# Buffers, queues and split places of the transform back in an S4 + MLP block

## The chip, the cores and the metric

One core of a Trainium2 chip runs the whole block in one program. The time is the device time of an execution in microseconds (us), read as the median of several runs. The engines named below are PE (TensorE), DVE (VectorE), ACT (ScalarE), POOL (GpSimd) and SP (SyncE, which here only issues DMAs). A DMA can be issued from SP, ACT or POOL; each has its own queue and issues in program order.

## The reference, cut to what matters

The block takes 2048 tokens of 512 channels, normalises and modulates them, and runs an S4 convolution (a kernel `K` per channel, applied by FFT of length 4096). A second normalisation and modulation is followed by a token-shift mixing (`w1`, gelu, four shifts, `w2`) and a channel MLP (`w3`, gelu, `w4`).

```python
x = A_u
h = layernorm(x) * (1 + ca) + sa
x = x + ga * S4(h)                       # y = irfft(rfft(K) * rfft(h)) + h * Dskip
h = layernorm(x) * (1 + cb) + sb
g = gelu(layernorm(h) @ w1)              # quarters of g shifted by +1, -1, +2, -2 tokens
x1 = h + shifted(g) @ w2
x = x + gb * (x1 + gelu(layernorm(x1) @ w3) @ w4)
```

## The kernel before

The program is written by hand in the order in which each engine runs it (`manual_schedule`); tiles come from pools with a fixed number of buffers, and an instruction that writes a new tile waits until the last use of the tile whose buffer it takes.

**Stage 1** (to about 209 us) computes the kernel `K` in SBUF (`KX`) and the first transform of `h`, which goes to DRAM as `VU`. Beside it POOL copies the weights from the inputs to DRAM scratch (`Dw2`, `Dw3`, `Dw4`).

**Stage 2** (about 209 to 302 us) is the middle of the transforms. `k_first` (eight rounds) makes `VK0` and `VK1`. Then come 16 steps, two halves `jh` of the channels with eight `kc` each. In step n, PE runs `spectrum_k(n)` (64 small products, reading the twiddles `T2` and the negated twiddles `T3`, which POOL writes in `flip`). DVE runs `multiply(n)`: four products (`ma`, `mb`, L690) and two sums (`zc`, L692). PE runs `back(n-1)` (four products with `Gm`); ACT evicts them to `z` (two buffers) and POOL stores `z` to DRAM (`ZT`, two DMAs of 256 KB). PE runs `spectrum_u(n+1)` on a block of `VU` (512 KB) that SP loaded into `ld`, a ring of seven buffers. The same ring holds the two loads of `w1` (512 KB each) and the blocks of the transform back, `load_inv`. SP also loads the four parts of `x` (1024 KB each) into `KX`. In steps 12 and 13 `inverse(0, 0)` and `inverse(0, 3)` use the first four loaded blocks of the first half (k = 0, 3, 4, 7), in step 15 `i1` uses the other four. `w1` and `w2` are split into a high part (ACT, L115) and a low part (DVE, L756) in steps 9, 10, 14 and 15.

**The hole** (about 302 to 314 us): after the last step the last `z` goes to DRAM and the blocks of the second half come back, transposed by the address pattern; only then can PE go on (`py`, L731).

**Stage 3** (about 314 to 374 us) is the rest of the transform back and the mixing. `mix_half(t, hl, hf)` does 24 products for half a pair of token tiles and gelu on ACT (`go`, two buffers), `mix_out` stores `go` to DRAM (`GD`), and `chan_load(g)` loads the shifted windows `win` from there. All these DMAs stand on SP's queue, and so do the loads of `w3` and `w4`. **Stage 4** (to the end) is the channel MLP, eight groups of tiles in `chan`.

## Time and profile before

| | |
|---|---|
| runs | 688.75, 689.73, 693.65 us; median 689.73 us |
| the profiled execution | 691.26 us, its span 689.5 us, mean clock 0.989 |
| PE busy | 642.6 us (93%) |
| DVE busy | 498.0 us (72%) |
| ACT busy | 331.2 us (48%) |
| POOL busy | 124.8 us (18%) |
| DMA | 86.42 MB, mean 125 GB/s |

PE's busy time is a sum over stages with different limits, and its matmuls overlap; the stages are read apart with the view by windows. A row of the timeline gives start, duration, engine, line, operation, output<-input and, in brackets, the idle time just before it and what ended it.

### The profile page before, as it was taken

The page shows a single profiled execution, that of the slowest core. Times are in us where ns is not written, and L with a number is a line of the kernel's source. Part 1 is how long each engine was busy: PE and PEld are TensorE (multiplying, and loading weights), DVE is VectorE, ACT ScalarE, POOL GpSimd, SP SyncE. Part 2 cuts the span into 40 slices and gives each one's busy share as a digit, 9 for nine tenths or more (in the row PEclk, how much of TensorE's full clock was granted, in tenths as well). Part 3 has the DMA queues.
Part 4 walks back from the last instruction along what each step waited for, and adds up shares of the span by engine and source line. Part 5 has one row for each costly group of instructions (what it writes and reads, how often), then busy time and mean ns, then how long its engine had stood idle before and what let it go on. Part 6 is the DMA issues. An engine that isn't in the chain of part 4 may idle for free.

```text
span 689.5 us, 16884 instructions
## 1 busy us (share of the span) xinstructions
PE 642.6 (93%) x7195; PEld 509.2 (74%) x7195; DVE 498.0 (72%) x795; ACT 331.2 (48%) x505; POOL 124.8 (18%) x236
## 2 busy tenths in 40 slices
PE   1899999999999998977998999999999999999996
PEld 0456655655569776634887889999899889898895
DVE  7899999999996887986987967464574536363522
ACT  3878988889875557432444623123131312222121
POOL 4011112112103355413741101001010000000000
PEclk9999999999999999998999999999999999999999
DMA  8603264643739997967387010020100201010001
GB/s 299 284 2 79 75 218 105 209 121 85 275 85 317 354 335 258 346 204 226 108 257 240 1 32 32 16 77 15 47 31 17 77 1 62 1 49 13 1 31 31
DMA packets 51091, 86.42 MB, mean 125 GB/s; under 512 B 4676, under 2 KB 39496, under 8 KB 48424
## 3 DMA queue, kind: packets, MB, share of 16 engines
q1 hardware_dynamic: 46712, 66.74, 30.1%
q0 software_dynamic: 3440, 17.57, 7.4%
q8 instruction: 56, 0.92, 0.6%
q10 hardware_dynamic: 864, 1.05, 0.5%
q14 instruction: 19, 0.16, 0.1%
HBM read 59.12 MB, written 32.90 MB: 133 GB/s over the span
## 4 chain that ended last, share of the span: by engine, by line
PE 70%; DVE 6%; DMA 5%; ACT 3%; POOL 2%; issue 1%; ACTq 0%; SPq 0%; DVEq 0%; POOLq 0%
PE pm L841 7%; PE pm L838 7%; PE pm L839 7%; PE xx L448 7%; PE pa L954 6%; PE pa L955 6%; PE pa L962 6%; PE kp L498 3%; DMA ZT<-z 3%; PE ph L893 2%; PE ph L895 2%; PE ph L892 2%; DMA ld<-ZT 2%; PE pu L426 2%; PE pT L803 2%; PE pk L626 2%
## 5 line engine op out<-in xcount | busy, mean ns | idle before, releaser
L115 ACT ACTIVATE gh<-pm 128x512 fp32r<-128x512 f32 (+1 forms) x48 | 26.9, 560 | 200.7 <-PE pm L841 200.7
L838 PE MATMUL pm<-nh,w3h 128*128 128x256 f32 (+1 forms) x352 | 86.6, 281 | 2.7 <-ACT nh L115 2.7
L839 PE MATMUL pm<-nh,w3l 128*128 128x256 f32 (+1 forms) x352 | 86.3, 280 | 0.1
L946 DVE TENSOR_TENSOR gl<-gf,gh 128x512 fp32r<-128x512 f32 (+1 forms) x48 | 30.8, 643 | 68.4 <-ACT gf L115 68.4
L954 PE MATMUL pa<-w4h,gh 128*128 128x512 f32 (+1 forms) x176 | 69.6, 395 | 0.0
L838 PEld LDWEIGHTS pm<-nh,w3h 128*128 128x128 f32 (+1 forms) x352 | 66.0, 187 | 4.4 <-ACT nh L115 2.9
L955 PE MATMUL pa<-w4l,gh 128*128 128x512 f32 (+1 forms) x176 | 68.9, 392 | 0.0
L839 PEld LDWEIGHTS pm<-nh,w3l 128*128 128x128 f32 (+1 forms) x352 | 65.9, 187 | 2.2 <-DVE w3l L756 0.5
L765 POOL TENSOR_TENSOR rs<-mv,eps_t 128x1 f32<-128x1 f32 (+1 forms) x39 | 11.0, 282 | 282.4 <-DVE mv L771 265.4
L841 PE MATMUL pm<-nl,w3h 128*128 128x256 f32 (+1 forms) x352 | 55.0, 278 | 0.0
L449 PE MATMUL xx<-MG,ON 64*128 64x512 f32 x160 | 48.1, 397 | 0.0
L962 PE MATMUL pa<-w4h,gl 128*128 128x512 f32 (+1 forms) x176 | 48.0, 390 | 0.0
L448 PE MATMUL xx<-MG,ON 64*128 64x512 f32 x160 | 48.0, 396 | 0.0
L841 PEld LDWEIGHTS pm<-nl,w3h 128*128 128x128 f32 (+1 forms) x352 | 47.0, 187 | 0.0
L898 DVE TENSOR_TENSOR h<-h,ph 128x512 f32<-128x512 f32 x16 | 11.0, 687 | 45.1 <-PE ph L895 45.1
L466 DVE SCALAR_TENSOR_TENSOR e<-tr,p 128x512 f32<-128x512 f32 x64 | 41.1, 684 | 1.5 <-ACT tr L115 1.5
L498 PEld LDWEIGHTS kp<-e,e 128*32 128x32 f32 x2048 | 30.1, 110 | 12.7 <-issue 7.6
L475 DVE TENSOR_TENSOR e<-tr,p 128x1024 f32<-128x1024 f32 x32 | 39.0, 1220 | 0.0
L476 DVE TENSOR_TENSOR e<-tr,m 128x1024 f32<-128x1024 f32 x32 | 39.0, 1219 | 0.0
L115 ACT ACTIVATE p<-xx 128x1024 f32<-128x1024 f32 (+1 forms) x40 | 37.5, 979 | 2.2 <-PE xx L252 1.0
L962 PEld LDWEIGHTS pa<-w4h,gl 128*128 128x128 f32 (+1 forms) x176 | 33.0, 188 | 7.3 <-DVE gl L946 0.2
L115 ACT ACTIVATE tr<-xx 128x1024 f32<-128x1024 f32 x32 | 33.0, 1030 | 9.6 <-PE xx L449 7.9
(236 smaller groups left out, 1731.6 us busy)
## 6 DMA issues: line engine op xcount, KB each, us to landing
VU<-vs SPq DMA_DIRECT2D x64, 128.0 KB, 3.7
ld<-VU SPq DMA_DIRECT2D x16, 512.0 KB, 7.4
ZT<-z POOLq DMA_DIRECT2D x30, 256.0 KB, 6.2
ld<-ZT SPq DMA_DIRECT2D x12, 512.0 KB
Dw<-in_w POOLq DMA_DIRECT2D x8, 688.0 KB, 4.7
xu<-in_u SPq DMA_DIRECT2D x4, 1024.0 KB, 8.0
KX<-in_x SPq DMA_DIRECT2D x4, 1024.0 KB, 8.0
GD<-go SPq DMA_DIRECT2D x16, 256.0 KB, 2.3
```

The costliest lines, as they stand in the source:

```text
L115: return S.activation(out, in_, f, bias=bias, scale=scale)
L448: T.matmul(x[:, :512], la, ma, start=(i == 0), stop=(i == len(ops) - 1))
L449: T.matmul(x[:, 512:], lb, mb, start=(i == 0), stop=(i == len(ops) - 1))
L466: V.scalar_tensor_tensor(e0[:, 1, a], tr[:, 1, 0], 1.0 - 2.0 * a, mg[:, a], op0=OP.mult, op1=OP.mult)
L475: V.tensor_mul(e0[:, 0], tr[:, 0, 0:1].to_broadcast([128, 2, 512]), mg)
L498: T.matmul(kp[32 * j:32 * j + 32, (k % 2) * 4 + g], e1[:, r, d], e0[:, r, :, d * 32:d * 32 + 32], start=(r == 0), stop=(r == 1), skip_grou ...
L838: T.matmul(p, wh[:, k, c], hi[k], start=(k == 0), stop=False)
L839: T.matmul(p, wl[:, k, c], hi[k], start=False, stop=False)
L841: T.matmul(p, wh[:, k, c], lo[k], start=False, stop=(k == 3))
L954: T.matmul(acc[i], gh[:m, e, s], W4h[:m, f], start=(f == 0), stop=False)
L955: T.matmul(acc[i], gh[:m, e, s], W4l[:m, f], start=False, stop=False)
L962: T.matmul(acc[i], gl[:m, e, s], W4h[:m, f], start=False, stop=(f == 10))
```

## The change

Six edits, all in stage 2 and around it. (1) `T3` becomes one tile for all twiddles, written by eight POOL instructions ahead of `k_first`; no flip is left in the 16 steps. (2) The `z` buffers go from two to three. (3) The ring `ld` goes from seven buffers to six, and the blocks k = 0, 3, 4, 7 of the first half get a pool of their own, `zi` (four buffers); they are loaded in step 9 instead of 10, the other four in step 12 instead of 13. `VU` is loaded four steps ahead instead of three. (4) The four loads of `x` move from SP's queue to POOL's, in the order 0, 3, 1, 2 in steps 2, 4, 6, 8. `FI` is loaded in `k_first` instead of step 9, and `Gm` takes `FK`'s buffer after `k_first`. (5) `w1` gets a DRAM copy too, is loaded by POOL straight into the tile of its low part in steps 9 and 10; ACT makes the high parts in steps 13 and 14, DVE the low parts in the hole. (6) `w2` is loaded by one SP DMA after the loads of the hole, its high part is made by ACT after `mix_half(1, hl, 0)`, its low part by DVE after `mix_half(2, hl, 0)`. The products on PE are the same.

```diff
-    Gm = c2.tile([128, 2, 64], F32, name="Gm")
-    ldp = a2.enter_context(pool("ldp", bufs=7))
+    ldp = a2.enter_context(pool("ldp", bufs=6))
...
-    def flip(kc):
-        t = t3s[kc] = c2.tile([128, 8, 64], F32, name="T3", bufs=3)
-        for gh in range(2):
-            r = slice(gh * 64, gh * 64 + 64)
-            P.tensor_scalar(t[r], T2[kc // 4][r, kc % 4 * 4:kc % 4 * 4 + 8, 64 - gh * 64:128 - gh * 64], -1.0, None, op0=OP.mult)
+    T3 = s2.tile([128, 32, 64], F32, name="T3", bufs=1)
+    def flip(i):
+        for a in range(0, 16, 8):
+            for gh in range(2):
+                r = slice(gh * 64, gh * 64 + 64)
+                P.tensor_scalar(T3[r, i * 16 + a:i * 16 + a + 8], T2[i][r, a:a + 8, 64 - gh * 64:128 - gh * 64], -1.0, None, op0=OP.mult)
...
-        z = s2.tile([128, 4, 256], F32, name="z")
+        z = s2.tile([128, 4, 256], F32, name="z", bufs=3)
...
-            zis[jh, k] = block()
+            zis[jh, k] = block() if jh or k in (1, 2, 5, 6) else zip_.tile([128, 4, 256], F32, name="zi")
...
     def load_x(g):
-        Y.dma_start(X2[:, g * 4:g * 4 + 4].rearrange("p b d -> p (b d)"), A["x"][g])
+        P.dma_start(X2[:, g * 4:g * 4 + 4].rearrange("p b d -> p (b d)"), A["x"][g])
...
             def split():
                 for j in range(m):
-                    h = hi[:n, i + j, c0:c1]
-                    act(h, w[:n, j])
-                    V.tensor_sub(lo[:n, i + j, c0:c1], w[:n, j], h.bitcast(F32))
+                    act(hi[:n, i + j, c0:c1], w[:n, j])
+                def low():
+                    for j in range(m):
+                        V.tensor_sub(lo[:n, i + j, c0:c1], w[:n, j], hi[:n, i + j, c0:c1].bitcast(F32))
+                return low
...
-            if n + 3 < 16:
-                load_vu(*steps[n + 3])
-            if n % 2 == 0 and n < 14:
-                flip(steps[n + 2][1])
-            if n in (3, 4, 6, 8):
-                load_x(n - 3 if n < 5 else n // 2 - 1)
+            if n + 4 < 16:
+                load_vu(*steps[n + 4])
+            if n in (2, 4, 6, 8):
+                load_x((0, 3, 1, 2)[n // 2 - 1])
+            if n in (9, 10):
+                w1s.append(ldw1(None, n % 9 * 2, 2, q=P))
+            if n in (13, 14):
+                w1s[n - 13] = w1s[n - 13]()
             if n == 9:
-                Y.dma_start(FI, A["FI"].rearrange("p (a b c) -> p a b c", a=32, b=2))
-            if split:
-                split()
-                split = None
-            if n in (8, 9):
-                split = ldw1(two, n % 2 * 2, 2)
-            if n == 10:
                 for k in (0, 3, 4, 7):
                     load_inv(0, k)
             if n == 12:
+                for k in (1, 2, 5, 6):
+                    load_inv(0, k)
                 inverse(0, 0)
-                w2s = [ldw2(None, 2 * i, 2) for i in range(2)]
...
-            if n in (14, 15):
-                w2s.pop()()
...
         for b in (14, 15, 4, 5, 6, 7):
             half_stat(b, 0)
+        for f in w1s:
+            f()
         for k in (1, 2):
             load_inv(1, k)
             load_inv(1, k + 4)
+        w2s = ldw2(None, 0, 4)
...
         mix_half(1, hl, 0)
+        w2s = w2s()
         mix_norm(2)
...
         mix_half(2, hl, 0)
+        w2s()
         chan_split(0)
```

On SP's queue in stage 2 (`VU` to `ld` are the blocks of u, `ZT_61` the first half's blocks of the transform back, `KX<-in_x` the parts of x), the last rows of the 16 steps stand so before:

```order
L724 DMA KX<-in_x 128x2048
L640 DMA ld<-VU 128x4x256 x2
L724 DMA KX<-in_x 128x2048
L750 DMA ld<-in_w 128x2x512
L640 DMA ld<-VU 128x4x256
L1131 DMA FI<-in_FI 128x2048
L750 DMA ld<-in_w 128x2x512
L640 DMA ld<-VU 128x4x256
L721 DMA ld<-ZT_61 128x4x256 x4
L640 DMA ld<-VU 128x4x256 x2
L750 DMA w2l<-Dw_64 128x2x512 x2
L721 DMA ld<-ZT_61 128x4x256 x4
```

And with the change, from the first block of `VU` on:

```order
L534 DMA xu<-in_T 128x2048
L640 DMA ld<-VU 128x4x256 x4
L1106 DMA FI<-in_FI 128x2048
L1108 DMA FK<-in_G 128x128
L640 DMA ld<-VU 128x4x256 x10
L721 DMA zi<-ZT_61 128x4x256 x4
L640 DMA ld<-VU 128x4x256 x2
L721 DMA ld<-ZT_61 128x4x256 x4
```

The loads of `x`, `w1` and `w2` are gone from this stretch of SP's queue; the first four blocks of `ZT_61` still stand ahead of the last two blocks of `VU`.

On POOL in the 16 steps (`T` are the negated twiddles, `ZT<-z` the stores, two to a step), before:

```order
L706 DMA ZT_61<-z 32x2x1024 x4
L662 TENSOR_SCALAR T_3646<-xu 64x512 x2
L706 DMA ZT_61<-z 32x2x1024 x4
L662 TENSOR_SCALAR T_3792<-xu 64x512 x2
L706 DMA ZT_61<-z 32x2x1024 x4
L662 TENSOR_SCALAR T_3949<-xu 64x512 x2
L706 DMA ZT_62<-z 32x2x1024 x4
```

And with the change:

```order
L662 TENSOR_SCALAR T_3079<-xu 64x512 x8
L706 DMA ZT_61<-z 32x2x1024 x4
L724 DMA KX<-in_x 128x2048
L706 DMA ZT_61<-z 32x2x1024 x4
L724 DMA KX<-in_x 128x2048
L706 DMA ZT_61<-z 32x2x1024 x4
L724 DMA KX<-in_x 128x2048
L706 DMA ZT_61<-z 32x2x1024 x4
L724 DMA KX<-in_x 128x2048
L706 DMA ZT_62<-z 32x2x1024 x2
L750 DMA w1l<-Dw_64 128x2x512
```

The flips between the stores are gone, and a load of `x` or `w1` stands in their place.

On ACT in the mixing (`go` are the gelus, `h` the normalised tiles, `nh` the high parts of the transposed tiles), around `mix_half(1, hl, 0)`, with the change:

```order
L115 ACTIVATE go<-pm 128x512
L115 ACTIVATE w2h<-w2l 128x512 x4
L115 ACTIVATE h_4961<-h_4961,nm,rs 128x512 x2
L115 ACTIVATE go<-pm 128x512
L115 ACTIVATE nh_5138<-pT_5128 128x512
```

Before, the row `w2h` does not stand there, and `h` follows the gelu.

## Rows read from the trace of the kernel before

**Rows 1.** View by windows, the head and five stretches
```profile
core 0: us, PE busy (x) PEld busy (x) DVE busy (x) ACT busy (x) POOL busy (x), PEclk, DMA share, GB/s
224.40:302.00 77.60, 70.45 (x1500) 52.08 (x1500) 67.30 (x112) 44.82 (x87) 35.15 (x42) 1.00 0.92 317
224.40:232.00 7.60, 7.12 (x178) 5.93 (x180) 5.38 (x9) 3.75 (x7) 0.00 (x0) 1.00 1.05 392
247.00:259.00 12.00, 12.00 (x273) 9.85 (x267) 11.77 (x20) 6.67 (x13) 8.52 (x10) 1.00 0.93 303
274.00:290.00 16.00, 13.65 (x278) 9.38 (x274) 16.00 (x28) 8.47 (x17) 9.04 (x11) 1.00 1.04 370
430.00:689.50 259.50, 253.88 (x1626) 228.85 (x1624) 125.81 (x208) 58.72 (x109) 14.02 (x36) 1.00 0.10 31
```

**Rows 2.** Timeline of DVE in the 16 steps
```profile
227.31 0.69 DVE L690 TENSOR_TENSOR ma<-pk,us 128x512 f32<-128x512 f32 x1 [2.12 <-PE pk L680]
...
238.42 0.69 DVE L690 TENSOR_TENSOR ma<-pk,us 128x512 f32<-128x512 f32 x1
...
245.29 0.69 DVE L690 TENSOR_TENSOR ma<-pk,us 128x512 f32<-128x512 f32 x1 [3.19 <-ACT us L115]
...
263.19 0.69 DVE L690 TENSOR_TENSOR ma<-pk,us 128x512 f32<-128x512 f32 x1 [2.69 <-ACT us L115]
...
271.48 1.29 DVE L756 TENSOR_TENSOR w1l<-ld,w1h 128x512 fp32r<-128x512 f32 x2 [1.01 <-ACT w1h L115]
...
276.55 1.70 DVE L756 TENSOR_TENSOR w1l<-ld,w1h 128x512 fp32r<-128x512 f32 x2
...
297.15 1.29 DVE L756 TENSOR_TENSOR w2l<-w2l,w2h 128x512 fp32r<-128x512 f32 x2 [0.26 <-ACT w2h L115]
...
301.36 0.69 DVE L692 TENSOR_TENSOR zc<-mb 128x512 f32<-128x512 f32 x1
```

**Rows 3.** Timeline of POOL, two pairs of flips
```profile
238.27 3.14 POOL L662 TENSOR_SCALAR T<-xu 64x512 f32<-64x512 f32 x2
...
256.72 3.10 POOL L662 TENSOR_SCALAR T<-xu 64x512 f32<-64x512 f32 x2
```

**Rows 4.** Timeline of ACT, two evictions to z
```profile
261.09 1.09 ACT L115 ACTIVATE z<-pz 128x512 f32<-128x512 f32 x2 [4.34 <-DMA ZT<-z]
...
268.38 1.08 ACT L115 ACTIVATE z<-pz 128x512 f32<-128x512 f32 x2 [1.93 <-DMA ZT<-z]
```

**Rows 5.** View of the tile ZT, 224 to 330 us, all its DMAs
```profile
DMA to landing us min/median/max: 2.6/6.0/8.9
```

**Rows 6.** Timeline of SP's queue, the first blocks of ZT
```profile
269.70 4.17 SPq L721 DMA_DIRECT2D ld<-ZT  x4
```

**Rows 7.** Chain of waits, the first use of these blocks
```profile
283.84 1.86 PE pz L731 x32
```

**Rows 8.** The page's DMA issues: KB each, median us to landing
```profile
KX<-in_x SPq DMA_DIRECT2D x4, 1024.0 KB, 8.0
```

**Rows 9.** Timeline of ACT in the mixing
```profile
348.54 1.72 ACT L115 ACTIVATE h<-h,nm,rs 128x512 f32<-128x512 f32 x2
350.81 0.60 ACT L115 ACTIVATE go<-pm 128x512 f32<-128x512 f32 x1 [0.55 <-PE pm L841]
...
374.67 2.20 ACT L115 ACTIVATE w4h<-w4l 128x512 fp32r<-128x512 f32 x4
```

**Rows 10.** Timeline of DVE in the mixing
```profile
357.91 1.22 DVE L879 TENSOR_TENSOR win<-win,wh 128x1024 fp32r<-128x1024 f32 x1 [2.46 <-ACT wh L115]
```

**Rows 11.** Timeline of PE, the first product of the MLP
```profile
374.37 0.58 PE L838 MATMUL pm<-nh,w3h 128*128 128x256 f32 x1 [2.69 <-ACT nh L115]
```

**Rows 12.** Chain of waits in the hole: start, duration, what
```profile
305.03 2.69 DMA ZT<-z
...
308.51 4.98 DMA ld<-ZT
```

**Rows 13.** Timeline of DVE in the hole
```profile
316.07 0.69 DVE L734 TENSOR_TENSOR KX<-py,KX 128x512 f32<-128x512 f32 x1 [7.69 <-PE py L731]
```

More of the change, by code (lines that the diff above doesn't have):

```diff
@@ L119, in body @@
     GD = dpool.tile([4, 128, 20, 128], F32, name="GD")
-    WD = {k: dpool.tile(list(A[k].shape), F32, name="D" + k) for k in ("w2", "w3", "w4")}
+    WD = {k: dpool.tile(list(A[k].shape), F32, name="D" + k) for k in ("w1", "w2", "w3", "w4")}
     ident = glob.tile([128, 128], F32, name="ident")
@@ L511, in body @@
     for k in range(2):
-        side[28 + 3 * k].append(lambda i=k * 256: P.dma_start(WD["w2"][i:i + 256], A["w2"][i:i + 256]))
+        for j, w in enumerate(("w1", "w2")):
+            side[24 + 4 * j + 2 * k].append(lambda w=w, i=k * 256: P.dma_start(WD[w][i:i + 256], A[w][i:i + 256]))
     for n in range(3, 6):
@@ L678, in spectrum_k @@
                             else:
-                                w = t3s[kc // 2 * 2][rows, k1 % 8]
+                                w = T3[rows, k1]
                             T.matmul(p[gh][kk * 64:kk * 64 + 64, i, ro], w,
@@ L1093, in split_w @@
         for _ in range(n):
-            splits.pop(0)()
+            splits.pop(0)()()
     steps = [(jh, kc) for jh in range(2) for kc in range(8)]
@@ L1099, in body @@
         flip(0)
-        Y.dma_start(Gm, A["G"].rearrange("p (a b) -> p a b", a=2))
+        flip(1)
         for r in range(8):
             k_first(r)
-            if r == 3:
-                load_vu(*steps[1])
+            if r in (1, 3, 5):
+                load_vu(*steps[r // 2 + 1])
             if r == 6:
-                load_vu(*steps[2])
+                Y.dma_start(FI, A["FI"].rearrange("p (a b c) -> p a b c", a=32, b=2))
+        Gm = pa12.tile([128, 2, 64], F32, name="FK")
+        Y.dma_start(Gm, A["G"].rearrange("p (a b) -> p a b", a=2))
         us = spectrum_u(*steps[0])
-        split = None
+        w1s = []
         for n, st in enumerate(steps):
@@ L1146, in body @@
                 inverse(0, 3)
-                for k in (1, 2, 5, 6):
-                    load_inv(0, k)
-            if n in (14, 15):
-                w2s.pop()()
         for f in i1:
@@ L1158, in body @@
         gop = ctx.enter_context(tp("gop", 2, side="right"))
+        pw2 = ctx.enter_context(tp("pw2", side="right"))
+        W2h, W2l, ldw2 = weights(pw2, WD["w2"], 512, 512, "w2", 4)
         psT = ctx.enter_context(tp("psT", space=PSUM))
```

15 lines of the change are left out of this document (6 added, 9 removed).

## The prediction

> **What bounds the kernel now.** I read the stages apart with the view by windows first. From 430 us on PE is busy 253.88 of 259.50 us [rows 1]: the MLP is PE's and the change doesn't touch it. The 16 steps are different: in 77.60 us DVE is busy 67.30, PE 70.45 (its matmuls overlap, so this is not its peak) and the DMA engines 0.92 of their time at 317 GB/s. So three resources are near their limits there, and the question is which of them waits. DVE's timeline answers: from 227.31 to 238.42, three steps, nothing waits and a step takes 3.70 us [rows 2]. All 16 take from 227.31 to 302.05 (the end of the last sum), 74.7 us, where 16 x 3.70 would be 59.2. What the reader is to see in rows 2 is that the difference stands there in a few places: two waits of 3.19 and 2.69 us for ACT's evictions, and the splits of w1 and w2, which DVE must do between two steps. Ahead of the first wait POOL's row shows a flip that ends at 241.41 [rows 3], the one that PE's products of step 4 read; ahead of the second a flip ends at 259.82, which step 8 reads. Behind the second wait an eviction also stood 4.34 us for the store of an older z [rows 4]: two z buffers and a store that lands after 6.0 us in the median and 8.9 at most [rows 5]. After the steps comes the hole, in which the last store (2.69) and the first load (4.98) follow one another [rows 12] and DVE idles 7.69 us [rows 13].
>
> **The change, part by part.**
>
> *Flips ahead, third z buffer.* The waits of 3.19 and 2.69 us go [rows 2]. A flip is 1.55 us [rows 3], so eight take 12.4 us on POOL from about 209 us, when stage 1 ends, to about 222; the first multiplication that needs them is fed just before 227.31, so they cost nothing. If POOL could start only 3 us later, they would end at 225 and still cost about nothing. A z is now reused after three steps: 11.1 us less some 1.5 for eviction and issue leaves a store 9.6 us, above the 8.9 of the slowest [rows 5].
>
> *Splits of w1 out of the steps.* DVE gets back 1.01 of waiting, 1.29 and 1.70 us [rows 2]. Its low parts come back as 2 x 1.29 = 2.6 us in the hole, beside 7.69 us of idle time [rows 13]: nothing, unless the hole shrinks below that. The high parts stay on ACT, two to a step, where ACT has 44.82 of 77.60 us busy [rows 1]: nothing.
>
> *Split of w2 out of the steps.* DVE gets back 0.26 + 1.29 us [rows 2]; the second w2 split ran after the last sum and gives nothing. Four conversions come back on ACT in the mixing, 2.20 us as the same four of w4 take [rows 9], between one gelu and the normalisation of the next tiles (1.72 us), which delays that and the gelu behind it. That gelu waited 0.55 us for PE anyway [rows 9], so 2.20 - 0.55 = 1.65 us are left, and PE waits for the high parts that follow. Would the wait of 2.69 us before the MLP [rows 11] swallow it? I think not: the store of the delayed gelu, the windows and the loads of w3 and w4 stand behind one another on SP's queue, so that wait moves along. Bounds 0 (swallowed) and 2.2; I take 1.7. DVE's four low parts, 2.6 us, fall into its idle 2.46 us before the split of the windows [rows 10], which itself comes 1.7 later: nothing.
>
> *Sum of what goes:* 3.19 + 2.69 + 1.01 + 1.29 + 1.70 + 0.26 + 1.29 = 11.4 us.
>
> *First blocks of the transform back.* This is where I expect a new wait. They could be loaded only when the last store of the first half had landed; that was at 269.70 [rows 6], and PE used them at 283.84 [rows 7], 14 us later. With the pace of 3.70 the store of z(7) is issued at about 227.3 + 8 x 3.7 + 2.5 = 259.4 and lands 6.0 us later [rows 5], at 265.4. Four blocks of 512 KB are 2.1 MB, at 370 GB/s [rows 1] 5.7 us: 271 if they are alone, 276.8 with the last x, one z and the first half of w1 (another 2.1 MB) ahead. PE wants them at 227.3 + 12 x 3.7 + 2.1 = 273.8. So between 0 and 3 us of waiting; I take the middle, 1.6.
>
> *The rest.* The ring has six buffers instead of seven: in the hole two blocks instead of one wait until PE has released the first ones, and 0.5 MB more takes some 1.5 us then; PE has work between, so 0 to 1, I take 0.2. The extra copy of w1 in stage 1 and Gm's late load (64 KB, wanted only after the first multiplication) are hidden by work of other engines; if that cover were gone, each would cost a DMA's landing, some 2 us. The load of w2 comes behind all loads of the hole on SP's queue and is wanted 30 us later: nothing. The hole keeps its length [rows 12].
>
> *Sum:* -11.4 + 1.6 + 1.7 + 0.2 = -7.9 us. On the profiled execution's 691.26 (span 689.5) that is 683.4; it lies 1.5 above the median of the runs, 689.73, so on the median 681.8, **682**.
>
> **Rivals.**
>
> *DMA becomes the bound.* From 224.4 us on the changed steps still move twelve blocks of u, fifteen z, four x, eight blocks of ZT and w1: 6.3 + 7.9 + 4.2 + 4.2 + 1.0 = 23.6 MB. My sum ends the steps at 302.05 - 9.8 = 292.2, 67.8 us for nearly all of this, 348 GB/s throughout. For it: rows with 392 and 370 GB/s [rows 1]. Against: 303 in the stretch from 247, with the engines 0.93 busy. At the mean of the steps before, 317, they need 74.4 us and end at 298.8: a gain of 3.2 less 1.9 for the mixing and the ring, 688.4. The Trainium skill, "DMA: Bandwidth & Descriptors", section "Specifications", gives a core about 358 GB/s of its memory; by it the steps would end at 290.3 at the earliest, which leaves the sum as it is but with 2 us to spare. The rows of 392 and 370 lie above that figure, so the measurement decides.
>
> *Slower: stores behind x on POOL's queue.* Each x of 1 MB now stands ahead of two stores in one queue. If a store waits for it whole, it lands after 8.0 [rows 8] + 6.0 [rows 5] = 14.0 us, where the third buffer leaves 9.6: 4.4 us of waiting behind each of four x, 17.6 us. With that, -11.4 + 17.6 + 1.6 + 1.9 = +9.7, 699.4. It decides from the point at which a store behind x takes more than 9.6 us; the change turns into a loss when the four cost 8 us together, 2 us each. Against it: DMA had to serve x and the stores at the same time before as well, and the slowest store took 8.9. The Trainium skill, same page, section "Queues, rings and completion order", says that every DMA engine goes round-robin between the queues that have work and in order within one: by it a store no longer overtakes an x that was issued before, which speaks against this change.
>
> *New waits don't come.* If the first blocks arrive in time and the 2.69 us before the MLP swallow ACT's four conversions, -11.4 + 0.2 gives 678.5.
>
> *It does not do what it says.* If the two large waits were caused by slow loads and not by flips and z buffers, they would stay (5.9 us) and the gain shrinks to 2.0: 687.7. Against it: each of the two flips ends some 3.5 us ahead of the late multiplication [rows 2, 3], the time that PE and ACT need between them. I count it with the DMA bound, whose time is the same.
>
> **How the numbers follow.** Forecast 0.50, DMA bound (with the last rival) 0.27, no new waits 0.16, slower 0.07. The forecast's own range is 679 to 684.5 (its three new waits all but gone, or all at their upper bounds, 3 + 2.2 + 1 = 6.2 us). The range for all goes from 678 (no new waits) to 689 (the DMA bound) and leaves out the slower case and some of the tails. One per cent, about what a measurement of this kernel can tell from no change, is 6.9 us, so faster means below 682.8. The forecast lies just inside: six in ten of its chance are below, and with all of "no new waits" and a little of the DMA bound that is 0.30 + 0.16 + 0.03 = 0.49 faster; slower 0.06; the rest, 0.45, within 1%.
>
> **What would show it.** Flips: no idle time of 3 us at step 4 and step 8 in DVE's timeline, and a step of 3.7 us through step 11. z buffers: no eviction that waits for ZT<-z. First blocks: a wait of PE for zi at step 12, 0 to 3 us. End of the steps at 291 to 294 us instead of 302.05, the hole 11 to 12 us as before. ACT's w2h in the mixing, and PE's start of the MLP at 374.4 - 9.8 + 1.9, about 366.5. It is wrong if stores take over 9.6 us behind x, if DVE's steps stretch evenly (DMA), or if the MLP starts later than 371.

## The result and the profile after

The changed kernel takes **692.75 us** in the median (690.80 to 696.13), the kernel before, on the same chip, 689.31: a ratio of 1.0044, with a 95% interval of 1.0029 to 1.0058. The forecast was 682.0 in a range of 678 to 689. So the change costs 3.4 us where 7.9 were to be gained, though by the measure of the prediction (within 1%) it is no change. The profiled execution has a span of 691.0 us; that of before had 689.5. The working below goes from span to span, 1.5 of the 3.4 us: the profiled execution of before lies 2 us above its kernel's median, that of the changed kernel (692.82) at its own.

The stages first. View by windows of the changed kernel, columns as in [rows 1]:

```profile
core 0: us, PE busy (x) PEld busy (x) DVE busy (x) ACT busy (x) POOL busy (x), PEclk, DMA share, GB/s
224.40:303.00 78.60, 66.54 (x1494) 51.81 (x1488) 62.14 (x105) 42.29 (x83) 19.57 (x36) 0.96 0.90 297
247.00:259.00 12.00, 11.02 (x259) 8.73 (x252) 10.08 (x18) 7.39 (x15) 3.79 (x7) 1.00 1.06 408
276.00:285.00 9.00, 0.99 (x18) 0.51 (x10) 2.98 (x5) 2.55 (x5) 1.07 (x2) 0.79 1.06 384
285.00:292.00 7.00, 6.63 (x120) 4.10 (x120) 4.06 (x9) 0.61 (x2) 0.00 (x0) 0.79 0.99 315
286.00:303.00 17.00, 16.86 (x345) 10.62 (x336) 14.46 (x26) 8.26 (x16) 2.84 (x6) 0.94 0.63 177
```

From DVE's first product to the end of its last sum the 16 steps take 76.6 us (226.76 to 303.35), 1.9 more than the 74.7 of before, though DVE works 5.2 us less in the stretch than in [rows 1]. From 276 to 285 PE is busy 0.99 of 9 us while the DMA engines are full, and after that DMA has room (0.63) while PE and DVE work: the two stand one behind the other instead of side by side. DVE's timeline shows where:

```profile
226.76 0.69 DVE L690 TENSOR_TENSOR ma<-pk,us 128x512 f32<-128x512 f32 x1 [2.11 <-PE pk L680]
...
275.30 0.69 DVE L690 TENSOR_TENSOR ma<-pk,us 128x512 f32<-128x512 f32 x1 [1.28 <-PE pk L680]
...
287.36 0.69 DVE L734 TENSOR_TENSOR KX<-pz,KX 128x512 f32<-128x512 f32 x1 [8.37 <-PE pz L731]
...
290.60 0.69 DVE L690 TENSOR_TENSOR ma<-pk,us 128x512 f32<-128x512 f32 x1
...
302.67 0.68 DVE L692 TENSOR_TENSOR zc<-mb 128x512 f32<-128x512 f32 x1
```

The same timeline of the kernel before has, for steps 12 and 13:

```profile
281.76 0.68 DVE L690 TENSOR_TENSOR ma<-pk,us 128x512 f32<-128x512 f32 x1
...
287.87 0.68 DVE L690 TENSOR_TENSOR ma<-pk,us 128x512 f32<-128x512 f32 x1
```

Step 12 begins 48.54 us after the first (before: 54.45), so the two long waits and the splits of [rows 2] are gone. But step 13 begins 15.30 us after step 12, where it was 6.11. The last sum of the steps begins at 302.67, against 301.36 in [rows 2]. PE's timeline has the other half, first the waits of PE in the steps, then the first product of the transform back:

```profile
255.31 1.09 PE L650 MATMUL pk<-ld,wm 64*64 64x256 f32 x16 [0.80 <-issue]
...
261.40 0.27 PE L680 MATMUL pk<-VK,T 64*64 64x128 f32 x1 [0.88 <-issue]
...
273.52 0.27 PE L680 MATMUL pk<-VK,T 64*64 64x128 f32 x1 [1.20 <-issue]
...
285.37 3.20 PE L731 MATMUL pz<-zi,FI 128*32 128x256 f32 x32 [8.38 <-DMA zi<-ZT]
```

A wait "<-issue" is one that no semaphore in the profile ends. The kernel before has none of over 0.1 us in its steps. The chain of waits (start, duration, what) leads from the wait at 285.37 back to the store of z(7), the last of the first half:

```profile
260.97 5.17 DMA ZT<-z
...
268.36 16.87 DMA zi<-ZT
285.37 3.20 PE pz L731 x32
...
292.20 1.86 PE pz L731 x32
```

The store lands at 266.1, as forecast (265.4). I call its landing the gate, since the first blocks can be loaded only from then on. The loads behind it take 16.87 us from the fourth issue and 19.1 from the gate, where I had 5.7 to 11.4 from the gate. And the 32 products behind the wait take 3.20 us, not 1.86 as in [rows 7] and again at 292.20: the granted clock from 285 to 292 is 0.79 in the mean, so part of the stretch runs at 1.2 of 2.4 GHz, after PE had stood for 8.4 us. Beyond the steps, from PE's timeline:

```profile
314.83 3.64 PE L731 MATMUL py<-ld,FI 128*32 128x256 f32 x32 [6.89 <-DMA ld<-ZT]
...
377.19 0.58 PE L838 MATMUL pm<-nh,w3h 128*128 128x256 f32 x1 [3.31 <-ACT nh L115]
```

The hole is as long as before: 12.16 us from the last sum to the first product of the second half, before 12.27 (to 313.63). From there to the MLP it is 62.36 us, before 60.74 to [rows 11]. The MLP itself takes 313.81 from 377.19 to the end, before 315.13.

### The profile page after: what moved, and what is told of

It reads as the page before. It is cut to its first block, busy times and chain, and to the rows that moved or that the text cites. A ratio compares the mean times of both kernels' runs of the same rounds, so it can differ in the third digit from the quotient of the medians.

```text
span 691.0 us, 16871 instructions
## 1 busy us (share of the span) xinstructions
PE 635.5 (92%) x7195; PEld 507.6 (73%) x7195; DVE 497.2 (72%) x795; ACT 331.2 (48%) x505; POOL 117.0 (17%) x236
## 4 chain that ended last, share of the span: by engine, by line
PE 59%; DVE 24%; DMA 8%; issue 3%; ACT 3%; POOL 1%; SPq 1%; ACTq 0%; DVEq 0%; POOLq 0%
PE pm L838 7%; PE pm L839 7%; PE pm L841 7%; PE pa L954 6%; PE pa L955 6%; PE pa L962 6%; DVE e L466 4%; DVE e L476 4%; DVE e L475 4%; PE pk L680 3%; DMA zi<-ZT 2%; DVE m L472 2%; PE ph L893 2%; PE ph L892 2%; PE ph L895 2%
## 5 line engine op out<-in xcount | busy, mean ns | idle before, releaser
L449 PE MATMUL xx<-MG,ON 64*128 64x512 f32 x160 | 47.1, 389 | 0.0
L448 PE MATMUL xx<-MG,ON 64*128 64x512 f32 x160 | 47.0, 389 | 0.0
## 6 DMA issues: line engine op xcount, KB each, us to landing
ZT<-z POOLq DMA_DIRECT2D x30, 256.0 KB, 6.3
GD<-go SPq DMA_DIRECT2D x16, 256.0 KB, 2.3
```

Of the source, the lines that this page charges most:

```text
L448: T.matmul(x[:, :512], la, ma, start=(i == 0), stop=(i == len(ops) - 1))
L449: T.matmul(x[:, 512:], lb, mb, start=(i == 0), stop=(i == len(ops) - 1))
```

## Experiments

Seventeen kernels, all but one edits of the changed kernel. The table has, for each, the start of step 12, PE's wait for the first blocks there, the starts of the last sum and of the first product after the hole (us in the profiled execution), the median time, and the ratio to the kernel before with its interval.

| run | step 12 | wait | last sum | after hole | median | ratio |
|---|---|---|---|---|---|---|
| before | 281.8 | none | 301.36 | 313.63 | 689.31 | |
| changed | 275.3 | 8.38 | 302.67 | 314.83 | 692.75 | 1.0044 [1.0029, 1.0058] |
| e1 x on SP | 275.8 | 7.79 | 303.54 | 315.71 | 693.54 | 1.0049 [1.0031, 1.0067] |
| e2 x2, w1 late | 273.3 | 4.34 | 298.30 | 310.30 | 689.27 | 0.9989 [0.9972, 1.0006] |
| e16 w1 late | 273.5 | 4.53 | 297.38 | 309.61 | 689.77 | 0.9994 [0.9970, 1.0018] |
| e9 no x | 271.9 | 7.81 | 299.55 | 311.76 | 689.36 | 0.9994 [0.9978, 1.0011] |
| e8 no gate | 276.5 | none | 295.12 | 307.63 | 686.07 | 0.9945 [0.9921, 0.9968] |
| e15 blocks on POOL | 276.4 | 4.18 | 300.89 | 313.66 | 688.94 | 0.9984 [0.9963, 1.0004] |
| e17 the same, x earlier | 275.7 | 4.82 | 301.21 | 313.45 | 690.13 | 1.0002 [0.9980, 1.0024] |
| e5 loads before the gate | 276.5 | 5.04 | 302.14 | 314.31 | 690.79 | 1.0031 [1.0012, 1.0050] |
| e3 late use | 273.9 | moved | 301.11 | 314.69 | 692.36 | 1.0030 [1.0010, 1.0051] |
| e6 u ahead, late use | 277.0 | none | 294.89 | 311.51 | 687.00 | 0.9976 [0.9957, 0.9996] |
| e11 e6, w1 in the hole | 275.9 | none | 293.39 | 313.78 | 687.98 | 0.9974 [0.9950, 0.9997] |
| e12 e11, last z first | 272.9 | none | 291.68 | 308.04 | 688.45 | 0.9978 [0.9958, 0.9998] |
| e18 combined | 277.7 | none | 296.28 | 314.86 | 688.29 | 0.9984 [0.9970, 0.9999] |
| e19 e18, last z first | 273.9 | moved | 296.51 | 310.62 | 688.84 | 0.9989 [0.9970, 1.0009] |
| e7 flips and z alone | 278.7 | none | 299.89 | 315.67 | 694.35 | 1.0079 [1.0060, 1.0098] |
| e14 flips in steps | 275.5 | 9.19 | 303.69 | 316.66 | 693.34 | 1.0059 [1.0041, 1.0076] |
| e4 w2 high early | 274.3 | 8.96 | 303.77 | 315.83 | 691.34 | 1.0034 [1.0016, 1.0052] |

One profiled execution differs from the median of its kernel by up to 5 us (e12: 683.79), so the columns of one row are read together and the ratio decides. The changed kernel and e4 are the same program up to the mixing, and e3 up to step 12. Their executions begin step 12 48.5, 47.4 and 47.6 us after the first, and the wait is 8.38 and 8.96, so differences of about 1 us between rows say nothing.

### What the first blocks wait for

**e1.** Loads of x back on SP's queue.

```diff
-        P.dma_start(X2[:, g * 4:g * 4 + 4].rearrange("p b d -> p (b d)"), A["x"][g])
+        Y.dma_start(X2[:, g * 4:g * 4 + 4].rearrange("p b d -> p (b d)"), A["x"][g])
```

> The changed kernel with one edit taken back: the four loads of x are issued by SP again, at the same places. Theory Q (what is served ahead of the first blocks of the transform back decides): in the changed kernel PE waited 8.4 us for them in step 12, with the last x (1 MB) issued at 261.5 behind a late eviction, 5 us ahead of them. SP reaches that x some 10 us earlier, while its own queue is nearly idle, so 1 MB less stands ahead: the wait falls by about 3 us to 5, the time to about 689.5. Theory B (the DMA engines are full, 23.6 MB decide, the order doesn't matter): the wait or another one of the same length stays, 692 to 693. Rival: x on SP's queue holds up the blocks of u behind it, new waits in steps 3 to 9, 694.

The wait is 7.79 us and the time that of the changed kernel: which queue carries x makes no difference here.

**e2.** The last x (group 2, "x2" in the expectations) at step 12 instead of 8, w1 two steps later.

```diff
-            if n in (2, 4, 6, 8):
-                load_x((0, 3, 1, 2)[n // 2 - 1])
-            if n in (9, 10):
-                w1s.append(ldw1(None, n % 9 * 2, 2, q=P))
-            if n in (13, 14):
-                w1s[n - 13] = w1s[n - 13]()
+            if n in (2, 4, 6, 12):
+                load_x({2: 0, 4: 3, 6: 1, 12: 2}[n])
+            if n in (11, 12):
+                w1s.append(ldw1(None, n % 11 * 2, 2, q=P))
+            if n in (14, 15):
+                w1s[n - 14] = w1s[n - 14]()
```

> The changed kernel with the last x moved from step 8 to step 12 and the two loads of w1 from steps 9 and 10 to 11 and 12 (their high parts from 13, 14 to 14, 15); the bytes are the same. Theory Q: 2.1 MB less are served ahead of the first blocks, 5.7 us at 370 GB/s, so the wait in step 12 falls from 8.4 to about 2.7 us and the time to about 687. Theory B: the wait moves to the other four blocks in step 15 or to the store of z, and the time stays at 692 to 693.

The wait is halved to 4.34 and the median falls by 3.5 us (3.8 by the ratios). Of the two loads that were moved, which one?

**e16.** w1 late as in e2, x as changed (the lines on w1 above alone).

> Changed kernel with w1's loads at steps 11 and 12 instead of 9 and 10 and its high parts at 14 and 15; x as changed. Without any x the wait for the first blocks was 7.81 us, with x2 and w1 both late 4.34. Theory S: w1 is what counted, since it was issued within 4 us of the first blocks, and x2 was served before they began; so the wait is 4 to 5.5 us here too and the time 689 to 690. Rival: neither alone does it: the wait stays at 7 to 8, 692.

w1 alone does it: wait 4.53, time 689.77, both as expected. The first product of PE, and then the DMA queues over the landing of the last block (266.8 to 279.6):

```profile
279.71 3.39 PE L731 MATMUL pz<-zi,FI 128*32 128x256 f32 x32 [4.53 <-DMA zi<-ZT]
```

```profile
DMA packets 3186, 4.53 MB, mean 354 GB/s; under 512 B 172, under 2 KB 2727, under 8 KB 3183
## 3 DMA queue, kind: packets, MB, share of 16 engines
q1 hardware_dynamic: 2628, 2.62, 62.6%
q0 software_dynamic: 555, 1.87, 37.1%
```

The same view of the changed kernel, 268.4 to 285.2:

```profile
DMA packets 3882, 5.88 MB, mean 350 GB/s; under 512 B 234, under 2 KB 3195, under 8 KB 3879
## 3 DMA queue, kind: packets, MB, share of 16 engines
q1 hardware_dynamic: 3047, 3.03, 56.4%
q0 software_dynamic: 832, 2.80, 42.8%
```

q1 is SP's queue, q0 POOL's. The rate is the same, 350 and 354 GB/s; what differs is how much of it POOL's queue takes. With 2.80 MB on q0 meanwhile the blocks land in 16.87 us, with 1.87 in 12.80. A longer landing also lets POOL move more in it, so these two points alone show no cause; that w1 is one is shown by the edit of e16. The engines serve both queues while both have work, so SP's loads are not behind POOL's stores and loads, nor ahead of them, but beside. The Trainium skill, "DMA: Bandwidth & Descriptors", section "Queues, rings and completion order", says the same (each engine goes round-robin between the queues that have work); the shares of 56 and 43% agree with it.

The mean hides how uneven the service is. From 274 to 278 us of the changed kernel SP's first blocks and POOL's stores and w1 are all under way:

```profile
q0 software_dynamic: 346, 1.21, 74.9%
q1 hardware_dynamic: 400, 0.39, 28.3%
```

The two queues get nearly the same number of packets, but POOL's are 3.5 KB in the mean and SP's 1.0 KB, so POOL's queue moves three quarters of the bytes. From 284 to 290, when POOL's queue moves nothing, SP's alone moves 2.10 MB, 350 GB/s, with the same small packets. This fits turns that are counted in packets and not in bytes; no run changed the size of a packet.

**e9.** No x at all: POOL fills its place with zeros, so x's part of the result is left out.

```diff
-        P.dma_start(X2[:, g * 4:g * 4 + 4].rearrange("p b d -> p (b d)"), A["x"][g])
+        P.memset(X2[:, g * 4:g * 4 + 4].rearrange("p b d -> p (b d)"), 0.0)
```

> Changed kernel without the four loads of x of 1 MB each: POOL fills those 4.2 MB with zeros instead, at the same places of the program, so x's part of the result is left out. PE's stalls of 0.6 to 1.8 us that no semaphore ends come every 6 to 7 us, each some 2.5 us after a 16 KB packet of the instruction queue began. Theory I (instructions wait behind data): with 4.2 MB less between 238 and 266 us the stalls up to 262 shrink below 0.3 each, steps 4 to 11 take 3.6 to 3.9, step 12 begins at 271 to 272 instead of 275.3; the gate opens 3 us earlier, the first blocks land in under 10 us without x2 beside them, and the wait of 8.38 falls to 1 to 4: 681 to 685. Rival (the stalls don't depend on the data traffic): they stay at 0.6 to 1.2, step 12 begins at 275, and only the landing of the first blocks gets shorter: 686 to 688.

Half of it came, and the time, 689.36, lies outside both ranges. Every stop "<-issue" of over 0.3 us is gone, steps 0 to 10 take 3.60 to 3.91 us each, and step 12 begins 45.5 us after the first, 3.0 earlier than in the changed kernel. But the wait stays at 7.81, so the loads of x were little or no part of it:

```profile
281.35 3.21 PE L731 MATMUL pz<-zi,FI 128*32 128x256 f32 x28 [7.81 <-DMA zi<-ZT]
```

In that landing (264.6 to 281.2) q0 moved 2.96 MB (z and w1), and it took 16.57 us: a third point beside 2.80 and 1.87.

**e8.** The first blocks are read from u's array, which is complete since stage 1, so they wait for no store; the transform back of that half then gets the wrong numbers.

```diff
-        q.dma_start(..., dram(ZT[jh], (k * 4 + a) * 32768, ...))
+        q.dma_start(..., dram(VU if not jh and k in (0, 3, 4, 7) else ZT[jh], (k * 4 + a) * 32768, ...))
```

> Changed kernel, except that the first blocks are read from u's array (complete since stage 1) instead of ZT, same bytes, same shape, so their loads wait for no store; what the transform back gives is left out of the meaning. Theory G: issued by 260 in place of 266.47 while the DMA has little to do, they land before 273, no wait at step 12, steps end near 294.5, 683 to 685. Rival R (rate): the 2.1 MB only change places with other loads; u of 11 to 14 or the z stores come late instead, steps end at 300 or later, 688 or more.

Issued from 253.5 on, the same bytes cost no wait, the last sum begins 7.6 us earlier and the time falls by 0.99% of before's against the changed kernel, 6.8 us. It comes 1 us above theory G's range and below rival R's. The landing is as slow (16.6 us); it no longer matters. So it takes both, the gate at 266 and the slow service behind it.

**e15, e17.** The blocks in POOL's queue ahead of w1 (the loads at step 9); e17 adds the last x at step 7 and the edit of e4.

```diff
-                    load_inv(0, k)
+                    load_inv(0, k, q=P)
-            if n in (9, 10):
-                w1s.append(ldw1(None, n % 9 * 2, 2, q=P))
+            if n in (10, 11):
+                w1s.append(ldw1(None, n % 10 * 2, 2, q=P))
...
-            if n in (2, 4, 6, 8):
-                load_x((0, 3, 1, 2)[n // 2 - 1])
+            if n in (2, 4, 6, 7):
+                load_x({2: 0, 4: 3, 6: 1, 7: 2}[n])
```

> Changed kernel with the loads of the first blocks issued on POOL's queue at step 9 instead of SP's, and w1's loads one step later (10 and 11), so behind them. Theory S (two queues share the DMA engines while both have work): from 264 to 280 what POOL issued (z, w1, x) took about half of the engines' time, so SP's 2.1 MB for the first blocks went at 100 to 170 GB/s and landed after 16.9 us. In POOL's queue they stand ahead of w1 and of the stores of later z, with only u of two steps on the other queue: they land in 6 to 9 us, at 273 to 276, the wait of 8.38 falls to 0 to 2 us, and the time is 683 to 686. A cost: the store of z(9) now stands behind them and lands 5 us later, within what the third buffer leaves. Rival B (sum of bytes): the engines have the same 5 MB to move whatever the order, the landing stays over 12 us, the wait over 5, 690 to 692.

> The run with the first blocks on POOL's queue, with the last x at step 7 instead of 8 and ACT's conversions of w2 moved up as in the earlier run on that (which gave 1.4 us). Theory S: 1.4 less than the run with POOL's queue alone and up to 1 more from the earlier x: 681 to 684, clearly faster than both kernels. Rival B: 688 to 690.

Both missed, and their times lie nearer to rival B: the wait only halves (4.18 and 4.82). The chain of e17 shows why:

```profile
269.62 2.17 POOL zi L721 x3
271.79 0.04 issue
271.83 0.04 POOLq L750
271.88 0.01 issue
271.88 10.59 DMA zi<-ZT
```

The store of z(7) landed at 268.97, not at 266.15, 8.3 us after its issue (260.64), the blocks were issued from 269.62 on, and SP, no longer held up, loaded the second blocks beside the first from 269.29 on.

**e5.** x one step earlier, w1 at steps 7 and 8, u of steps 14 and 15 ahead of the blocks, and the edit of e4.

```diff
-            if n + 4 < 16:
-                load_vu(*steps[n + 4])
-            if n in (2, 4, 6, 8):
-                load_x((0, 3, 1, 2)[n // 2 - 1])
-            if n in (9, 10):
-                w1s.append(ldw1(None, n % 9 * 2, 2, q=P))
+            for m in {9: (13, 14, 15)}.get(n, (n + 4,) if n < 9 else ()):
+                load_vu(*steps[m])
+            if n in (1, 3, 5, 7):
+                load_x((0, 3, 1, 2)[n // 2])
+            if n in (7, 8):
+                w1s.append(ldw1(None, n % 7 * 2, 2, q=P))
```

> Changed kernel with x one step earlier each (steps 1, 3, 5, 7), w1 two steps earlier (7, 8), u of steps 14 and 15 ahead of the first blocks on SP's queue, and ACT's conversions of w2 moved as in the run before on that. Theory G (gate and order): the first blocks cannot start before the last store of the first half lands, 266.15; what was issued behind that point (x, w1, u14, u15: 3.1 MB) shared the DMA with them for 16.87 us. Moved ahead of the gate it fills stretches that moved 200 to 306 GB/s. Then the blocks land about 7 us after issue, at 273 to 274, the wait of 8.38 falls to 0 to 1 us, the steps end near 295, and with 1.4 from w2 the time is 682 to 684. Rival R (rate): the DMA engines are at their limit all along, so the moved bytes delay u and z there: steps 4 to 9 take 2 to 4 us longer, the steps end at 299 or later, 687 to 689.

Missed as well, for the reason seen in e17: what is moved ahead of the gate runs beside the store of z(7) and delays the gate itself. From its issue (261.61) to the first load behind it (270.38) it is 8.8 us here, 7.7 in e6, 9.2 and 9.5 in e11 and e12, 4.4 in e9 without x, 6.0 in the changed kernel. Rival R of that expectation was nearer (687 to 689 forecast, 690.79 measured).

### Where the wait goes when the use is later

**e3.** First blocks used at steps 14 and 15. **e6** adds u of 14 and 15 ahead of them and the edit of e4; **e11** is e6 with w1 loaded at steps 13 and 14, split in the hole, and the last x at step 7; **e12** is e11 with the last transform of the steps ahead of the products of the transform back; **e18** is e6 with only u of step 14 ahead and w1 as in e2; **e19** is to e18 what e12 is to e11.

The late use (e3 and all others here):

```diff
             if n == 12:
                 ...
+                pass
+            if n == 14:
                 inverse(0, 0)
                 ...
-            if n == 13:
+            if n == 15:
                 inverse(0, 3)
```

u ahead in e6, e11 and e12, and in e18 and e19:

```diff
-            if n + 4 < 16:
-                load_vu(*steps[n + 4])
+            for m in {9: (13, 14, 15)}.get(n, (n + 4,) if n < 9 else ()):
+                load_vu(*steps[m])
```

```diff
+            for m in {9: (13, 14), 11: (15,)}.get(n, (n + 4,) if n < 9 else ()):
+                load_vu(*steps[m])
```

w1 in the hole (e11, e12), and the last z first (e12, e19):

```diff
-            if n in (9, 10):
-                w1s.append(ldw1(None, n % 9 * 2, 2, q=P))
-            if n in (13, 14):
-                w1s[n - 13] = w1s[n - 13]()
+            if n in (13, 14):
+                w1s.append(ldw1(None, n % 13 * 2, 2, q=P))
...
         for f in w1s:
-            f()
+            f()()
```

```diff
+        back(*steps[15])
         for f in i1:
             f()
-        back(*steps[15])
```

> The changed kernel with the products of the first blocks (and their sums and statistics) moved from steps 12 and 13 to steps 14 and 15; no DMA is moved. If the wait is only a matter of when they are wanted (they landed at 285.2, step 14 would begin about 283.7): no wait over 2 us, about 685.5. Theory B: PE waits 5 us or more at another place (a block of u in step 13 or the other four blocks in step 15), 690 to 693.

> Changed kernel, all loads of x and w1 as they are; u of steps 14 and 15 ahead of the first blocks on SP's queue, the first blocks used at steps 14 and 15 instead of 12 and 13, ACT's conversions of w2 moved. Theory G: the blocks land at 283 to 285 as before, but nobody wants them until step 14, which begins at 283 at a pace of 3.7 from 275.3: a wait of 0 to 2 us in place of 8.38, none for u14; steps end near 296, time 683 to 685. Rival R: with the wait gone the bytes are simply not there in time; PE waits for u12, u13 or the second blocks (ld) instead, the steps end after 300 and the time is 688 to 690.

> The run with u ahead and late use (687.0), with w1's two loads at steps 13 and 14 instead of 9 and 10, both parts of its split in the hole, and the last x at step 7 instead of 8. Theory G: 1 MB less stands between the gate and the second blocks, which landed at 295.5 and made PE wait 2.94; that wait goes, and the steps end 2 to 3 us earlier: 683 to 685. Rival: w1 now shares the hole with the last store and the first loads, which lengthens it by 1 to 2 us, so nothing is left: 686 to 688.

> As the run with w1 in the hole, and the last transform of the steps (back of step 15, whose store opens the hole) stands ahead of the products of the transform back on PE instead of behind them. The eviction of the last z waited until 301.24, 6 us after its last sum at 294.9. Theory: its store is issued 2 to 3 us earlier, and the products that stood ahead fill PE's wait of 6.9 us: the hole ends 2 to 3 us earlier, 681 to 683. Rival: the hole is set by what DMA still has to do, and PE's wait for the last sum ahead of the products costs what the store wins: within 1 us of the run without it.

> Changed kernel with what the earlier runs pay for: w1's loads at steps 11 and 12 with the high parts at 14 and 15 (wait 8.38 to 4.53), the first blocks used at steps 14 and 15, u of step 14 alone ahead of them on SP's queue (u of both made the store that they wait for land after 7.7 to 8.9 us instead of 5.7), ACT's conversions of w2 moved up. Theory: the first blocks land at 278 to 280, nobody waits for them; the second blocks, behind 9.5 MB that must be moved after the gate at some 370 GB/s, land at 291 to 294 and cost 0 to 3 us: steps end at 293 to 295, 684 to 687. Rival: the same sum with a wait of 4 us or more for the second blocks, 688 to 690.

> The combined run with the last transform of the steps ahead of the products of the transform back on PE. Here w1 is split before the hole, so PE's dummy products don't wait for it as they did (4.68 us) in the earlier run of this order. Theory: the last store leaves 2 to 3 us earlier and the wait for the second blocks lies beside it: 2 us less than the combined run, 682 to 685. Rival: what DMA still has to move sets the hole: within 1 us of the combined run.

In e3 the wait moves to u of step 14, whose load stands behind the blocks in SP's queue. PE's timeline of e3:

```profile
287.64 1.99 PE L650 MATMUL pk<-ld,wm 64*64 64x256 f32 x16 [8.12 <-DMA ld<-VU]
```

That is theory B of that expectation, in wait and time. With u ahead (e6) no load is waited for at steps 12 to 14; PE then waits 2.94 us for the second blocks, and 687.00 is 0.68% of before's time below the changed kernel. e11 and e18 bring the steps' end to 293 and 296 and wait 4.64 and 2.84 us for these same blocks. In e19 two loads are waited for, as its PE timeline shows:

```profile
287.18 1.99 PE L650 MATMUL pk<-ld,wm 64*64 64x256 f32 x16 [3.92 <-DMA ld<-VU]
...
294.78 1.93 PE L731 MATMUL pk<-ld,FI 128*32 128x256 f32 x32 [0.54 <-DMA ld<-ZT]
```

So the five with u ahead end within 2 us of one another, 687.0 to 688.8, with another load as the last one: between the first load behind the gate (267 to 269 us) and about the end of the steps DMA moves 8.7 MB in e6, 8.3 in e12, 9.6 in e18 and 9.2 in e19, at 305 to 339 GB/s, which takes 24 to 30 us. What they win at the last sum goes again in the hole, which is 14.1 to 20.4 us long in them (12.16 in the changed kernel): in e6, e11 and e18 the wait for the second blocks now stands behind that sum, ahead of the last store, and in e11 and e12 PE waits 4.68 us there for the high part of w1. No theory's range (681 to 687) was reached; in e11, e12, e18 and e19 the rival's time came. e12 gained nothing over e11 in the median, as its rival said. e6, e11, e12 and, barely, e18 are faster than both kernels by their intervals, by 0.16 to 0.26% against the kernel before.

### Whether the removed waits were worth what was taken

**e7.** The kernel *before* with the flips ahead, three z buffers, six in the ring and Gm late, and nothing else; T3 and flip are those of the change.

```diff
+    T3 = s2.tile([128, 32, 64], F32, name="T3", bufs=1)
-    ldp = a2.enter_context(pool("ldp", bufs=7))
+    ldp = a2.enter_context(pool("ldp", bufs=6))
-        z = s2.tile([128, 4, 256], F32, name="z")
+        z = s2.tile([128, 4, 256], F32, name="z", bufs=3)
         flip(0)
+        flip(1)
-            if n % 2 == 0 and n < 14:
-                flip(steps[n + 2][1])
```

> Kernel before with the flips ahead, three z buffers, the ring of six and Gm late; loads, w1, w2 and the first blocks as before. The prediction's terms for these are 3.19 + 2.69 less 0.2: 5.7 us, which on 689.5 gives 683.8. Theory G: both waits go, but z(7) lands only some 5 us earlier while the steps want the first blocks 6 us earlier, and the wait of 1.86 for them at step 12 grows by 1 to 3 us: 685 to 687. Rival R: all of it comes back as waits for DMA: 688.5 or more.

It is 5.4 us **slower** than the kernel before, far above what the prediction's terms and theory G give. Rival R (688.5 or more) has the time, but what came back is only in part a wait for DMA that the profile shows. The profiled executions are 2.9 us apart (spans 692.4 and 689.5); the rest is that before's lies above its median, so no row shows it. Both waits are gone and step 12 begins 51.8 us after the first (before 54.5), but PE now stops five times for nothing that the profile shows. PE's timeline of e7:

```profile
244.31 0.44 PE L649 MATMUL pk<-ld,wm 64*64 64x256 f32 x3 [0.68 <-issue]
250.67 0.33 PE L679 MATMUL pk<-VK,xu 64*64 64x128 f32 x3 [1.36 <-issue]
257.61 1.09 PE L649 MATMUL pk<-ld,wm 64*64 64x256 f32 x16 [0.94 <-issue]
263.69 0.27 PE L679 MATMUL pk<-VK,T 64*64 64x128 f32 x1 [0.87 <-issue]
...
301.39 3.33 PE L730 MATMUL pk<-ld,FI 128*32 128x256 f32 x32 [4.78 <-DMA ld<-ZT]
```

The fifth, 0.99, ends at 269.48; together they are 4.84 us, and of the 5.88 that were removed 2.7 are left at step 12. Steps 12 to 13 then take 7.63 us (before 6.11). Behind the last sum the second blocks are waited for (4.78, before 1.48), since their loads were issued from 288.0 on instead of 283.9, and the hole is 15.8 us long instead of 12.3.

**e14.** The changed kernel with the flips back in the steps.

```diff
-        flip(1)
+            if n % 2 == 0 and n < 14:
+                flip(steps[n + 2][1])
```

> Changed kernel with the flips back in the steps, one every second step, as in the kernel before; everything else as changed. The prediction gave their removal 3.19 us and a share of the 2.69: by it this is 3 to 6 us slower, 696 to 699. Theory C (the waits covered others): the stops for flips give the instruction fetch and the DMA engines time that the steps otherwise lose as PE stalls and as the wait for the first blocks; PE's stalls go down by 2 to 3 us, the wait at step 12 from 8.4 to 4 to 6, and the time is within 1 us of 692.7.

693.34, within 1 us of the changed kernel, and the intervals overlap. Four stops for flips (0.53 to 0.54 each on PE) are back, and of PE's three stops "<-issue" of over 0.25 us one is left (1.47). Theory C held in that; the wait for the first blocks did not shrink as it said (9.19).

### w2

**e4.** ACT's conversions of w2 one block earlier in the mixing.

```diff
         hl = parts_of(transposed(mh.pop(0)[0]))
+        w2s = w2s()
...
         mix_half(1, hl, 0)
-        w2s = w2s()
```

> The changed kernel with ACT's four conversions of w2 moved from behind the gelu of tile 1 to behind the conversions of tile 0, where ACT idled 3.5 us in the kernel before. If they cost PE 1.6 us in the mixing, as PE's waits at 352.8 to 354.6 say: 1.6 us faster, 691.1, and these waits gone. If the wait before the MLP had swallowed them: the same time, 692.7.

691.34, 1.4 us less than the changed kernel by the medians and 0.7 by the ratios, whose intervals overlap. From the first product after the hole to the MLP the profile has 60.14 us instead of 62.36. One pair overstates it: over all traces this stretch takes 61.2 to 62.4 us where the conversions stand as changed (nine kernels, mean 61.8) and 60.1 to 61.7 where they are moved up (eight, mean 60.7). So the term is real, and about 1 us. In the changed kernel it stands on ACT between the gelu and the normalisation:

```profile
349.87 2.18 ACT L115 ACTIVATE w2h<-w2l 128x512 fp32r<-128x512 f32 x4
351.95 1.51 ACT L115 ACTIVATE h<-h,nm,rs 128x512 f32<-128x512 f32 x2
```

## Why the prediction was wrong, point by point

**The step that failed is "First blocks of the transform back".** Its term was 1.6 us, with bounds of 0 and 3; it measured 8.38, and 0.8 more for what ran at half clock behind it (15.30 against 6.11 is 9.19 in all). The mechanism, a new wait of PE for zi at step 12, and its gate, z(7)'s landing (265.4 forecast, 266.1 measured), were right. The size was not: I let the four blocks go at the full rate, 370 GB/s, with at most 2.1 MB "ahead" of them, and had them landed by 276.8; they landed at 285.2. Of the 350 GB/s that there were, SP's queue got 180 (3.03 MB in 16.8 us), because POOL went on issuing z and w1 beside it. The blocks are 2.1 of these 3.03 MB, some 125 GB/s; the rest is what SP had issued behind them. e16 takes w1 away and gets 3.9 us of the wait back; e8 takes the gate away and gets all of it.

**The pace of 3.70 failed too**, and it stood in the sums of two steps without a term of its own. It was read from three steps, 227 to 238, and laid over twelve (undisturbed, as in e9, steps of 3.60 and 3.91 take turns, 3.76 in the mean). To step 12 the change gained 5.91 of the 9.88 us of waits and splits; the missing 4.0 are four waits of DVE for PE (0.64, 1.27, 0.90, 1.28) that go with PE's stops "<-issue". So "nothing waits" was true of these three steps, of PE too, and did not hold for the later ones. In e7, with the waits gone and the loads as before, such stops appear, and in e14, with the flips back, most of them go again. In e9 they vanish with 4.2 MB of DMA traffic. That is one execution: e11 and e12 are the same program up to the last step, and PE stops in e11 at 249.6 and 256.0 us, but in e12 not before 259.

**Right:** flips and z. No idle time of 3 us at steps 4 and 8, no eviction that waits for ZT<-z, no cost of the flips in stage 1; but more than half of what they gave by step 12 went to PE's stops, so the terms of 3.19 and 2.69 were no gain in the time (e7, e14). **Right:** the splits of w1 and w2 (from step 13 to the last sum it is 1.42 us less, forecast 1.55), the low parts in the hole (free), the hole's length (12.16 against 12.27). **Right in kind:** w2 in the mixing, 62.36 less 60.74 = 1.6, forecast 1.7; that this pair meets the forecast so closely is in part luck, since all traces together give about 1 us (e4). **Not foreseen:** 1.3 us that the MLP gives back. That the steps begin 0.55 earlier is scatter: in the variants they begin between 225.2 and 228.0.

From span to span: to the first step -0.55, to step 12 -5.91, step 12 +9.19, to the last sum -1.42, hole -0.1, mixing +1.6, MLP -1.3: +1.5, which is 691.0 less 689.5.

**The rivals.** "DMA becomes the bound" (688.4) was nearest: when the wait at step 12 is taken away by a later use, the next load is waited for, and those versions measure 687.0 to 688.8. e8 is the exception: with no gate it moves its bytes at 339 GB/s from 254 to 296 us and no load of the steps is waited for (686.07). The rival's own sign, steps that stretch evenly, didn't come. What it lacked is that a stop for DMA in the middle is worse than a stretch throughout: in the changed kernel DMA falls to 177 GB/s from 286 on, because the last stores hang on the steps that the wait held up. "Stores behind x" did not come as told: no z buffer was late, and the slowest store landed after 8.1 us, where 9.6 were the limit. But the store of z(7) does land later when more is issued beside it (4.4 to 9.5 us to the first load), and that store is the gate. "No new waits" was wrong in its premise. Of the signs that the prediction named for being wrong, one came: the MLP starts at 377.2, later than 371.

**Left open.** That PE's stops are its instruction stream waiting behind data is supported, not shown by an experiment of its own: see the last section. Why the second blocks are loaded 4.1 us later in e7, which lengthens its hole, wasn't tried; the ring of six is one candidate.

## What to carry to other kernels

A pace read from the first undisturbed steps is the best that the others can reach. Waits that are removed from a stretch whose DMA engines are over 0.9 busy can have been covering others, so ask what gets its time there, and test the removal alone before the rest is built on it. For a load that stands behind a gate, reckon with the share of the rate that its queue will get while the other queue keeps issuing, not with the whole rate, and count the bytes that must follow the gate: in the five versions with u ahead their order changed the time by less than 2 us. Moving other loads ahead of the gate delayed the store that opens it (6.0 us to 7.7 and more).

## What was not expected of the hardware

PE stops of 0.3 to 2.3 us, often some 6 us apart, that no semaphore ends. In e7 the instruction queue moves one packet at a time, and five of them begin at 242.0, 248.1, 255.0, 261.3 and 267.0 us (to 0.1 us); PE goes on at 244.31, 250.67, 257.61, 263.69 and 269.48, each time 2.3 to 2.6 us later. The DMA view of 242.0 to 242.1 and of 248.1 to 248.2 has, for that queue (packets, MB, share of 16 engines):

```profile
q8 instruction: 1, 0.02, 67.4%
```

```profile
q8 instruction: 1, 0.02, 68.8%
```

In all nineteen traces together PE stops so 70 times by over 0.2 us (226 to 300 us), and every one of these stops ends 2.2 to 3.3 us after such a packet began. Not every packet has a stop behind it: 67 of the 118 that begin between 240 and 280 us have one.

The Trainium skill, "Runtime: NRT & Kernel Launch", section "Instruction fetch mechanics", says that the instruction memory is refilled in blocks of 16 KiB over a DMA queue of the sequencer's own, and that crossing a block is mostly hidden. With the DMA engines 0.94 to 1.06 busy it was not hidden here; in e9, with 0.79 to 0.95 from 235 to 271 us, it was but for 0.29 us. But the packets themselves take about as long in e9 (0.9 to 1.4 us after 240) as in the changed kernel (0.9 to 1.7). So what decides whether PE has to stop is open.

After PE had stood for 8.4 us the granted clock was 0.79 in the mean of the next 7 us, and the same 32 products took 3.20 us instead of 1.86: a stop of PE costs more than its length.

The MLP is 1.3 us shorter (313.81) than before (315.13). In the other kernels with w2 loaded in the mixing it lasts 313.6 to 314.8, in e7, which loads it in the steps, 315.0; why, no run shows.
